# An attention and mixer kernel on one Trainium2 core: the second channel matrix of group 0 converted one run earlier, twenty unread products at the start, and two rewritten order tables

## The chip, the cores and the metric

The kernel runs on one core of a Trainium2 chip. The metric is device time in microseconds (us), the median of three executions. One further execution was recorded by the hardware profiler, and all rows below come from it. The engines are named as in the profile: PE is TensorE, DVE is VectorE, ACT is ScalarE, POOL is GpSimd, SP issues most of the DMAs.

## The reference

Rotary attention over 4 batches of 8 heads (576 rows, 64 dimensions, fp32), followed by a token mixer and a channel mixer:

```python
q_rot, k_rot = (rotate(q), rotate(k))              # 4 x 8 x 576 x 64
scores = scale * np.matmul(q_rot, k_rot.transpose(0, 1, 3, 2))
attn = np.exp(scores - max); attn = attn / (sum + 1e-09)
x = concat_heads(attn @ v)                         # 4 x 576 x 512
h = np.maximum(xt @ w_tok1, 0.0) @ w_tok2          # 576 -> 256 -> 576, float64 weights
u = x + h.transpose(0, 2, 1)
h2 = np.maximum(u @ w_ch1, 0.0) @ w_ch2            # 512 -> 1536 -> 512, float64 weights
return (u + h2).astype(np.float32)
```

## The kernel before, in words

**Attention.** Heads go in 16 pairs; pair n is prepared by `prep(n)`. The rows of k and q are loaded by SP, rotated in three operations (L437, L439, L443: on DVE for pair 0, in two parts; on POOL for the others), transposed on PE with the identity `ident` (L471, PSUM tiles `s`) and copied to `kt` and `qt` (L482). The scores (L593) take 288 of the 576 columns at a time; DVE finds the maximum (L493), ACT takes the exponential (L497), PE transposes the result (L616), L621 copies it to `pt`, L634 multiplies by v. The last 64 rows of two neighbouring pairs are done together as tails (L516 for their scores), so the tails of pairs 0 and 1 need both pairs' `kt` and `qt`. X and XT hold the attention's output, scaled at L668 and its neighbours.

**The mixers.** A float32 matrix that enters a product here is split into a high and a low part and multiplied three times. The weights arrive as float64 in 32-bit halves and are rebuilt by `f64_split`, one piece at a time: two ACT operations (L709, L711), a clamp L713 (DVE or POOL), L715, L717 and L719 on DVE, L721 and L723 (DVE or POOL), then L729 on ACT for the high and L730 (DVE or POOL) for the low part. The token mixer is L819 (first product), L824 and L827 (its result split into `rs`), L841 (second product) and L844 (addition to X); L791 and L793 split X into `xs` and `xt` ahead of it. The channel mixer works on four groups of 384 hidden columns. Each of five chunks of rows is transposed once (`up`: L910 on PE, ACT L915 gives `uh`, DVE L916 gives `ul`), and then for every group and chunk `cm1` (L936, then `gh` by ACT L938 and `gl` by DVE L940) and `cm2` (L963, added to X by DVE at L965). `cm1` needs the first matrix of its group (`c1h`, `c1l`), `cm2` the second (`c2h`, `c2l`).

**What sets the order.** The code records tasks with an engine, a model duration and their dependencies, and three calls of `plan.run` issue them. Run 1 (attention, the token weights, the token mixer of batch 0) follows the table `ORDER1`, one number for each task. Run 2 (the token mixers of batches 1 to 3, the first matrix of group 0, `up(0)` and `up(1)`) follows `ORDER2`. Run 3 (the second matrix of group 0, all other weights, `up(2)` to `up(4)`, `cm1`, `cm2`) is list-scheduled by the planner from its model durations. Each engine executes its own queue strictly in order. PSUM has eight banks, `s` in run 1 and `m` in runs 2 and 3; a product can start only when the reader before it has released its bank.

Of the kernel before, what the change touches and what calls it, by code (L numbers as in the profile page):

```python
# [64 lines left out]

class Task:
# [8 lines left out]
class Plan:  # L75
# [53 lines left out]
    def place(self, t, s, eng, dur, fn):  # L129
# [13 lines left out]
        fn()  # L143
# [3 lines left out]
        self.clock[eng] = end  # L147
# [64 lines left out]
AT = {'load': [1.46, -95.74, 1755.84, -446.16, -10.32, -39.47], 'rot': [-30.33, -28.71, -413.29, -24.98], 'pt': [2461.71, -120.88, 1877.09, 0.03], 'qk': [-19.92, -94.77, -29.81, -42.47, -64.18, 1974.42, -445.69, 27.95, -11.96, -66.6, -413.71, -4.28, -3.14, 1684.05, 2036.62, 1632.15, 1700.12, -3.39, -14.08, 1717.83], 'mx': [-18.32, -97.08, -28.47, -222.21, 6.35, 102.54, -32.49, -15.54, 1579.98, 1593.71, -66.46, 1669.44, -16.89, 1934.18, 1942.38, -85.25, -54.68, -66.81, 1912.69, -8.83, 1697.35, 2415.63, 1609.9, 23.08, -40.85, -271.23, 8.19, -10.94, -20.04, -405.36, -59.72, -406.05, 2099.98, 1.92, 1651.83, 1951.2, 1677.89, 1499.17, -7.34, 1632.2], 'ex': [-19.75, -25.79, -97.92, -19.73, 1983.61, 1573.24, -17.98, -1.23, -9.94, -101.57, 88.51, 1713.87, -29.01, 1630.6, -9.17, 1879.5, 1922.03, -18.78, -23.18, 19.55], 'tr': [-261.73, 1684.38, -347.64, 1853.57, -223.18, 1740.33, -18.09, 1625.16, -353.85, 2050.66, -65.51, 2482.09, -74.23, -25.76, 1924.68, -6.29, -550.16, 2116.11, -49.33, -19.36], 'cp': [-285.8, 1993.92, -15.28, -338.61, -33.12, -32.9, 1494.57, -414.57, -230.35, -354.01, -214.2, -9.85, -35.68, -247.66, -14.87, -307.76, -26.24, 90.92, 1865.89, 2189.31], 'pv': [1983.73, 10.91, -453.58, -23.11], 'p1': [-52.7, -56.83, 1864.91, -1.75], 'fin': [2216.99, -20.0], 'tok': [1652.21, 1875.86, 1482.41, 2166.22, -11.87, 1947.96], 'inv': [-8.92, -3.44], 'f6': [1767.81, 1652.44], 'tk': [1968.59, -7.94, -26.45, -12.06], 'pre': [-2.55], 'tm': [-283.71, 77.1, 1499.3, -17.97, 1601.75, -59.36, 1543.29, -96.53, -111.26, 1974.16, 1626.79, -49.74], 'wg': [1621.69], 'up': [3.65, 1617.77], 'ti': [5.61]}  # L212
ORDER1 = (
# [848 lines left out]
```

## Time and profile before

| | |
|---|---|
| device time, median of 3 | 602.62 us (602.53 to 603.88) |
| the profiled execution, device time | 602.69 us |
| its span in the trace | 600.9 us (1.8 us lie outside it) |
| PE busy | 585.6 us, 97% of the span |
| DVE, ACT, POOL busy | 385.3, 312.4, 309.3 us |
| run 1 to run 2 on PE | at 252.8 us |
| run 2 to run 3 on PE | at about 295 us |

The page of the profile gives busy time by engine, and the granted clock of PE. The view of waits sums PE's idle time by the instruction that ended it. The timeline lists starts and durations, and in brackets the idle time ahead of an instruction and its releaser. In this program a float32 product leaves two records for each instruction in the order, one for each pass; a transpose leaves one. Durations of single PE records overlap their neighbours, so what PE pays is the distance between starts.

### The profile page before, as it was taken

What the parts mean: (1) busy time and instruction counts of PE and PEld (TensorE: products, weight loads), DVE (VectorE), ACT (ScalarE), POOL (GpSimd) and SP (SyncE); (2) the same over time, 40 slices, a digit from 0 to 9 for tenths busy, and PEclk for the clock granted to TensorE, in tenths of its full rate; (3) what the DMA queues carried; (4) which work ended last, traced back from release to release, by engine and by line L of the source; (5) the groups of instructions that cost most, each with busy time, mean ns of one, the idle gap of its engine ahead of it and who ended that gap; (6) DMA issues with size and microseconds to landing.
All of it is one profiled execution on the core that took longest, in us unless ns stands there. A gap on an engine that the chain in (4) does not pass through costs nothing.

```text
span 600.9 us, 12684 instructions
## 1 busy us (share of the span) xinstructions
PE 585.6 (97%) x4825; PEld 461.0 (77%) x4825; DVE 385.3 (64%) x1121; ACT 312.4 (52%) x796; POOL 309.3 (51%) x258
## 2 busy tenths in 40 slices
PE   4999999999999999999999999999999999999997
PEld 3777676777677777687777888888888888888886
DVE  6998999998899988688845545445423443223232
ACT  3998999999999988243464332233202311110110
POOL 4997876888868531023578686477503760000000
PEclk9999999999999999999998999999999999999999
DMA  5443242313311201001122222122101200001123
GB/s 151 126 116 86 71 108 75 105 29 90 101 52 60 62 2 31 25 26 62 36 65 76 71 61 54 60 71 55 50 1 36 71 0 1 1 1 70 71 70 106
DMA packets 34093, 36.15 MB, mean 60 GB/s; under 512 B 13808, under 2 KB 27632, under 8 KB 34032
## 3 DMA queue, kind: packets, MB, share of 16 engines
q1 hardware_dynamic: 33200, 35.01, 20.3%
q8 instruction: 38, 0.62, 0.4%
q10 hardware_dynamic: 832, 0.33, 0.2%
q14 instruction: 23, 0.19, 0.1%
HBM read 30.61 MB, written 4.72 MB: 59 GB/s over the span
## 4 chain that ended last, share of the span: by engine, by line
PE 95%; DVE 2%; DMA 1%; ACT 1%; issue 0%; DVEq 0%
PE m L936 25%; PE m L963 24%; PE s L634 14%; PE s L593 11%; PE s L616 7%; PE m L841 3%; PE m L819 3%; PE s L471 2%; PE s L516 2%; PE s L819 1%; PE s L537 1%; PE s L663 1%; PE s L841 1%; DMA tabs<-in_tab_dram 1%; DVE p L493 0%; DMA kraw<-in_k_dram 0%
## 5 line engine op out<-in xcount | busy, mean ns | idle before, releaser
L938 ACT ACTIVATE gh<-m 128x512 fp32r<-128x512 f32 (+1 forms) x60 | 33.3, 555 | 174.0 <-PE m L936 170.8
L497 ACT ACTIVATE p<-p,nm 128x576 f32<-128x576 f32 x128 | 98.9, 778 | 1.7 <-DVE p L493 1.1
L940 DVE SCALAR_TENSOR_TENSOR gl<-m,gh 128x512 fp32r<-128x512 f32 (+1 forms) x60 | 38.1, 637 | 93.3 <-ACT gh L938 93.2
L965 DVE TENSOR_TENSOR X<-m,X 128x512 f32<-128x512 f32 (+1 forms) x65 | 44.4, 683 | 74.0 <-PE m L963 73.9
L936 PE MATMUL m<-uh,c1h 128*128 128x512 f32 (+1 forms) x240 | 89.1, 371 | 0.1
L936 PE MATMUL m<-ul,c1h 128*128 128x512 f32 (+1 forms) x240 | 88.9, 370 | 0.0
L936 PE MATMUL m<-uh,c1l 128*128 128x512 f32 (+1 forms) x240 | 88.9, 370 | 0.0
L634 PE MATMUL s<-pt,vraw 128*64 128x256 f32 (+1 forms) x640 | 84.7, 411 | 0.0
L963 PE MATMUL m<-c2l,gh 128*128 128x512 f32 (+1 forms) x219 | 84.6, 386 | 0.0
L963 PE MATMUL m<-c2h,gh 128*128 128x512 f32 (+1 forms) x219 | 84.6, 386 | 0.0
L963 PE MATMUL m<-c2h,gl 128*128 128x512 f32 (+1 forms) x219 | 84.6, 386 | 0.0
L593 PE MATMUL s<-kt,qt 64*128 64x288 f32 x512 | 80.9, 430 | 1.2 <-ACT kt L482 0.9
L721 POOL TENSOR_TENSOR fa<-fc,fa 128x512 f32<-128x512 f32 (+2 forms) x30 | 35.9, 1197 | 75.2 <-DVE fa L719 63.4
L634 PEld LDWEIGHTS s<-pt,vraw 128*64 128x64 f32 x640 | 43.1, 137 | 30.1 <-DVE p L493 1.3
L493 DVE TENSOR_SCALAR_CACHE_REDUCE p<-s,nm 128x288 f32<-128x288 f32 x128 | 62.3, 512 | 3.8 <-PE s L593 1.7
L621 ACT COPY pt<-s 128x320 f32<-128x320 f32 (+1 forms) x172 | 60.6, 408 | 4.9 <-PE s L616 3.4
L616 PEld LDWEIGHTS s<-ident,p 64*128 64x128 f32 x1152 | 47.0, 139 | 17.5 <-ACT p L497 8.1
L593 PEld LDWEIGHTS s<-kt,qt 64*128 64x128 f32 x512 | 51.1, 192 | 8.7 <-ACT pt L621 1.7
L493 DVE TENSOR_SCALAR_CACHE_REDUCE p<-s 128x288 f32<-128x288 f32 x128 | 53.9, 452 | 4.4 <-PE s L593 4.0
L713 POOL TENSOR_SCALAR fa<-fa 128x512 f32<-128x512 f32 (+3 forms) x30 | 50.9, 1699 | 9.5 <-ACT fa L709 9.4
L616 PE MATMUL s<-ident,p 64*128 64x64 f32 x1152 | 52.6, 226 | 0.3 <-ACT p L497 0.2
L936 PEld LDWEIGHTS m<-uh,c1h 128*128 128x128 f32 x240 | 45.5, 190 | 8.1 <-DVE ul L916 0.3
(130 smaller groups left out, 1061.8 us busy)
## 6 DMA issues: line engine op xcount, KB each, us to landing
stg<-in_moe_w_ch_dram SPq DMA_DIRECT2D x16, 384.0 KB, 3.2
stg<-in_moe_w_ch_dram SPq DMA_DIRECT2D x12, 512.0 KB, 3.7
vraw<-in_v_dram SPq DMA_DIRECT2D x16, 256.0 KB, 3.2
kraw<-in_k_dram SPq DMA_DIRECT2D x15, 256.0 KB, 3.2
qraw<-in_q_dram SPq DMA_DIRECT2D x15, 256.0 KB, 3.3
out_dram<-X SPq DMA_DIRECT2D x15, 256.0 KB, 2.3
stg<-in_moe_w_tok_dram SPq DMA_DIRECT2D x4, 512.0 KB, 4.3
kraw<-in_k_dram SPq DMA_DIRECT2D x32, 32.0 KB, 2.9
```

The source lines that it names most:

```text
L493: return lambda: nc.vector.tensor_scalar(out=p()[:, c * W2:(c + 1) * W2], in0=sb.t[:, 0:W2], scalar1=-D ** -0.5, scalar2=nm.t[:, 0:1] if c ...
L497: return lambda: nc.scalar.activation(out=p(), in_=p(), func=ACTF.Exp, bias=nm.t[:, 1:2], scale=-1.0, accum_out=l())
L593: nc.tensor.matmul(sbs[h].t[:, 0:W2], flat(qt.t)[halves[h], TL + j * P:TL + (j + 1) * P], flat(kt.t)[halves[h], TL * (1 - h) + u * W2:TL * ...
L616: nc.tensor.transpose(xy[z].t[:, i * TL:(i + 1) * TL], pb.t[halves[z], c0:c0 + P], ident[halves[z], halves[z]])
L621: return lambda: e(out=pt[c].t[:, R * h:R * h + m, o + z * TL:o + (z + 1) * TL], in_=xy[z].t[:, 0:m * TL].rearrange("p (r s) -> p r s", r=m))
L634: nc.tensor.matmul(ab.t[halves[h], 0:w], vb.t[:, h, r, :], m, start=(r == 0), stop=(r == R))
L713: clamp = lambda e: lambda: e.tensor_scalar(out=A(), in0=A(), scalar1=EXP_LO, scalar2=EXP_HI, op0=ALU.max, op1=ALU.min)
L721: mul_ = lambda e: lambda: e.tensor_tensor(out=A(), in0=C(), in1=A(), op=ALU.mult)
L936: nc.tensor.matmul(tb.t[:, 0:n], a, m, start=(i == 0), stop=(i == len(lst) - 1))
L940: y = add("DVE", dve(n), lambda f=f, tb=tb: nc.vector.scalar_tensor_tensor(out=gb.t[1][:, f, 0:n], in0=tb.t[:, 0:n], scalar=0.0, in1=gb.t[ ...
L963: nc.tensor.matmul(tb.t[:, 0:w], a, m, start=(i == 0), stop=(i == len(lst) - 1))
L965: y = add("DVE", dve(w) + 0.08, lambda u=u, tb=tb, cols=cols, w=w: nc.vector.tensor_tensor(out=u[:, cols], in0=tb.t[:, 0:w], in1=u[:, cols ...
```

## The change

Four things are changed in what runs, and a fifth is added that does not run.

- `make_identity` is called ahead of the POOL fills of `vraw`, `oT` and `pq` instead of behind them.
- A function `warm(n, w)` issues 2n products of the identity with itself into PSUM banks 7 and 6; nothing reads them. `warm(10, P)` is called ahead of the first `prep`. A second call stands inside the closure `tr` under a condition on `nm`. The closure is executed after the loop over `nm`, when `nm` is `"v"`, so the condition is never met.
- `weights(0, ..., (2,), held)`, the conversion of group 0's second matrix (three pieces), is recorded ahead of `plan.run(ORDER2)` instead of behind it. `ORDER2` grows from 162 to 195 entries, and run 3 has 33 tasks fewer and is scheduled anew.
- `ORDER1` is another permutation of the same 1666 tasks, and `ORDER2` is rewritten.
- Code that can merge two PSUM banks (`Half`, `duo`, `mx1`, `cq1`, `cp1`, `f51`) is added. It acts on the numbers in `MERGED`, and `MERGED` is empty.

```diff
+MERGED = ()
 ORDER1 = (
-    68, 84, 0, 16, 88, 8, 20, 24, 28, 36, 4, 92, 12, 96, 104, 40, 44, 48, 76, 100, 52, 64, 72, 60, 80, 108, 112, 116, 148, 156, 152, 32, 56, 1408, 1428,
+    68, 0, 84, 16, 20, 88, 24, 92, 96, 100, 28, 12, 4, 8, 40, 32, 44, 104, 48, 52, 64, 60, 56, 72, 80, 76, 36, 1464, 108, 112, 116, 120, 132, 128, 1472,
...
+        make_identity(nc, ident)
         for _, _, t in raw["v"].free:
             nc.gpsimd.memset(t[TL:P, 0, R, :], 0.0)
...
-        make_identity(nc, ident)
+
+        def warm(n, w):
+            for i in range(2 * n):
+                z = halves[i % 2]
+                nc.tensor.matmul(banks.tile[:, 7 - i % 2, 512 - w:512], ident[z], ident[z, 0:w], start=True, stop=True)
...
+                        if n == 0 and nm == ("q" if r0 == 0 else "k"):
+                            warm(2, TL)
...
+        warm(10, P)
         for n in range(NP):
             prep(n)
...
             ups[ci] = up(ci, AT["up"][ci])
+        weights(0, AT["wg"][0] + 1000, (2,), held)
         plan.run(ORDER2)
...
         held[0].users -= 1
-        weights(0, 1000, (2,), held)
         for ci in range(2, NC):
             ups[ci] = up(ci, 1000 + 100 * ci - 120)
```

How many instructions of each line an engine has is the same on PE but for the twenty products. Lines of the changed kernel are higher by 33 to 72: L471 is L504 there, L593 is L648, L616 is L674, L516 is L566, L910 is L982, L916 is L988, L936 is L1008, L963 is L1035, L965 is L1037, and L715, L717, L719 are L787, L789, L791.

The first rows on PE, before (the numbers behind names are buffers; `uk` and `uq` are the rotated rows of pair 0, `p` the exponentials):

```order
L471 MATMUL s<-ident,uk_105 128x64 x4
L471 MATMUL s<-ident,uq_106 128x64 x4
L471 MATMUL s<-ident,uk_105 128x64 x6
L593 MATMUL s<-kt_109,qt_112 128x288 x6
L471 MATMUL s<-ident,uq_106 128x64 x6
L593 MATMUL s<-kt_109,qt_112 128x288 x2
L616 MATMUL s<-ident,p_115 128x64 x8
L593 MATMUL s<-kt_109,qt_112 128x288 x8
```

and now:

```order
L415 MATMUL s<-ident 128x128 x20
L504 MATMUL s<-ident,uq_106 128x64 x4
L504 MATMUL s<-ident,uk_105 128x64 x10
L648 MATMUL s<-kt_109,qt_112 128x288 x2
L504 MATMUL s<-ident,uq_106 128x64 x6
L648 MATMUL s<-kt_109,qt_112 128x288 x12
L504 MATMUL s<-ident,uk_105 128x64 x10
L648 MATMUL s<-kt_109,qt_112 128x288 x2
```

Twenty products stand ahead of the first transposes, and the other rows up to the first tails (L516, now L566) are the same in number, in another sequence.

On PE in run 3, where the transposes of chunks 2 to 4 begin (eighty in a row in both kernels), before:

```order
L936 MATMUL m_3981<-ul_3992,c1h_3985 128x512
L936 MATMUL m_3981<-uh_3991,c1l_3986 128x512
L910 MATMUL m_3984<-ident,XT_63 128x64
L910 MATMUL m_3983<-ident,XT_63 128x64
L910 MATMUL m_3984<-ident,X_61 128x64
```

and now:

```order
L1035 MATMUL m_4004<-c2h_4007,gh_4413 128x512
L1035 MATMUL m_4004<-c2l_4008,gh_4413 128x512
L1035 MATMUL m_4004<-c2h_4007,gl_4414 128x512
L982 MATMUL m_3999<-ident,XT_63 128x64
L982 MATMUL m_4000<-ident,XT_63 128x64
L982 MATMUL m_3999<-ident,X_61 128x64
```

The eighty transposes stood behind `cm1` of chunks 0 and 1; now `cm2` of chunks 0 and 1 stands between, and they come 72 products later.

On DVE at the same place, before:

```order
L940 SCALAR_TENSOR_TENSOR gl_4361<-m_3981,gh_4360 128x512
L916 TENSOR_TENSOR ul_3994<-m_3984,uh_3993 128x8x64
L717 SCALAR_TENSOR_TENSOR fh_70<-stg_66,fa_68 128x512
L916 TENSOR_TENSOR ul_3994<-m_3983,uh_3993 128x8x64
L719 TENSOR_SCALAR fa_68<-fh_70 128x512
L916 TENSOR_TENSOR ul_3994<-m_3980,uh_3993 128x8x64
L916 TENSOR_TENSOR ul_3994<-m_3982,uh_3993 128x8x64
L916 TENSOR_TENSOR ul_3996<-m_3979,uh_3995 128x8x64
```

and now:

```order
L1037 TENSOR_TENSOR X_60<-m_4002,X_60 128x512
L1037 TENSOR_TENSOR X_60<-m_4004,X_60 128x512
L789 SCALAR_TENSOR_TENSOR fh_69<-stg_65,fa_68 128x512
L988 TENSOR_TENSOR ul_4014<-m_3999,uh_4013 128x8x64
L988 TENSOR_TENSOR ul_4014<-m_4000,uh_4013 128x8x64
L988 TENSOR_TENSOR ul_4014<-m_3998,uh_4013 128x8x64
L988 TENSOR_TENSOR ul_4014<-m_4003,uh_4013 128x8x64
L988 TENSOR_TENSOR ul_4016<-m_3997,uh_4015 128x8x64
```

Two conversion steps stood between the first three `ul`; now one stands ahead of the first, and eight `ul` follow without a break.

## Rows read from the trace of the kernel before

**Rows 1.** The page, busy us (share of the span) and instructions of each engine.
```profile
PE 585.6 (97%) x4825; PEld 461.0 (77%) x4825; DVE 385.3 (64%) x1121; ACT 312.4 (52%) x796; POOL 309.3 (51%) x258
```

**Rows 2.** PE's waits: releaser, us in total, times, longest us.
```profile
PE s L471 <- DVE uk L443: 7.2, 2, 6.0
PE m L910 <- DVE ul L916: 1.7, 3, 0.9
PE m L819 <- DVE X L668: 1.3, 1, 1.3
```

**Rows 3.** Timeline of the start: start us, us, engine, line, output, count, idle before.
```profile
5.99 0.48 PE L471 MATMUL s<-ident,uk 64*128 64x64 f32 x4 [5.99 <-DVE uk L443]
...
9.35 1.81 PE L593 MATMUL s<-kt,qt 64*128 64x288 f32 x6 [0.87 <-ACT kt L482]
...
10.31 1.54 POOL L437 TENSOR_TENSOR w<-kraw,tabs 128x640 f32<-128x640 f32 x1 [7.58 <-DMA kraw<-in_k_dram]
...
18.05 1.55 POOL L443 TENSOR_TENSOR uq<-uq,w 128x640 f32<-128x640 f32 x1
...
19.80 0.75 PE L471 MATMUL s<-ident,uq 64*128 64x64 f32 x10
...
20.66 0.49 DVE L482 COPY qt<-s 128x320 f32<-128x320 f32 x1 [0.18 <-PE s L471]
...
21.26 1.20 PE L516 MATMUL s<-kt,qt 64*64 64x288 f32 x16
```

**Rows 4.** PE records of L593 from 9 to 14 us, and from 14.3 to 16.
```profile
L593 PE MATMUL s<-kt,qt x16: 684/684/847, 9.3 to 13.3; 64*128 64x288 f32 x16
...
L593 PE MATMUL s<-kt,qt x13: 402/402/507, 14.4 to 15.9; 64*128 64x288 f32 x13
```

**Rows 5.** Timeline where run 1 ends on DVE and run 2 begins on PE.
```profile
251.05 1.27 DVE L844 TENSOR_TENSOR X<-s,X 128x512 f32<-128x512 f32 x2
...
252.80 0.70 PE L819 MATMUL m<-xs,w1h 128*128 128x512 f32 x2 [1.27 <-DVE X L668]
```

**Rows 6.** Windows of run 2 (252.8 to 292.8 us): busy time by engine, summed over four.
```profile
sum 40.00, PE 40.00 PEld 32.18 DVE 34.17 ACT 16.51 POOL 11.40; mean PE 10.00 PEld 8.05 DVE 8.54 ACT 4.13 POOL 2.85
```

**Rows 7.** DVE groups of 252.8 to 330 us: busy us, mean ns of one, idle before.
```profile
L793 DVE TENSOR_TENSOR xs<-X,xs 128x512 fp32r<-128x512 f32 x9 | 6.9, 779 | 0.7 <-ACT xs L791 0.6
...
L791 DVE CAST xs<-X 128x512 fp32r<-128x512 f32 x6 | 2.6, 425 | 1.8 <-PE m L819 1.7
...
L715 DVE TENSOR_SCALAR fa<-fa 128x512 uint32<-128x512 uint32 x3 | 2.0, 680 | 1.1 <-POOL fa L713 1.1
...
L717 DVE SCALAR_TENSOR_TENSOR fh<-stg,fa 128x512 uint32<-128x512 uint32 x3 | 2.0, 682 | 0.0
...
L719 DVE TENSOR_SCALAR fa<-fh 128x512 uint32<-128x512 uint32 x3 | 1.2, 419 | 0.0
```

**Rows 8.** Timeline of the eighty transposes in run 3 and what DVE does meanwhile.
```profile
311.58 0.28 PE L910 MATMUL m<-ident,XT 64*128 64x64 f32 x2
...
312.31 0.69 DVE L940 SCALAR_TENSOR_TENSOR gl<-m,gh 128x512 fp32r<-128x512 f32 x1 [1.32 <-ACT gh L938]
...
313.56 0.68 DVE L717 SCALAR_TENSOR_TENSOR fh<-stg,fa 128x512 uint32<-128x512 uint32 x1
...
314.75 0.42 DVE L719 TENSOR_SCALAR fa<-fh 128x512 uint32<-128x512 uint32 x1
...
315.09 4.99 DVE L916 TENSOR_TENSOR ul<-m,uh 128x512 fp32r<-128x512 f32 x10
...
317.02 0.19 PEld L936 LDWEIGHTS m<-uh,c1h 128*128 128x128 f32 x1 [0.27 <-DVE ul L916]
```

**Rows 9.** Windows about that place: us, PE busy (records), granted clock, DMA share, GB/s.
```profile
314.00:317.70 3.70, 1.87 (x18) 1.00 0.44 111
317.80:321.10 3.30, 3.30 (x9) 0.50 0.00 0
321.20:325.00 3.80, 3.80 (x18) 1.00 0.39 104
```

More of the change, by code (lines that the diff above doesn't have):

```diff
@@ L63, in t, with __init__ @@
         return self.held[2]
+class Half:
+    def __init__(self, buf, z):
+        self.buf = buf
+        self.z = z
+    @property
+    def t(self):
+        return self.buf.t[:, self.z]
 class Task:
@@ L142, in place @@
                 b.slots.taken += 1
-        fn()
+        if fn:
+            fn()
+        else:
+            end = -1e9
         t.end, t.eng = end, eng
@@ L146, in place @@
             self.mode = t.mode
-        self.clock[eng] = end
+        self.clock[eng] = max(self.clock[eng], end)
         if eng == "DVE" and t.port:
@@ L392, in attention, with duo, none @@
             nc.gpsimd.memset(t[:, S:S + TL], 0.0)
-        make_identity(nc, ident)
+        def warm(n, w):
+            for i in range(2 * n):
+                z = halves[i % 2]
+                nc.tensor.matmul(banks.tile[:, 7 - i % 2, 512 - w:512], ident[z], ident[z, 0:w], start=True, stop=True)
         ready, ready_v, couple = {}, {}, {}
+        duos = [0]
+        def duo():
+            duos[0] += 1
+            if duos[0] - 1 in MERGED:
+                b = Buf(banks, True)
+                return b, [Half(b, 0), Half(b, 1)]
+            return None, [Buf(banks), Buf(banks)]
+        def none(deps, bufs):
+            return add("DVE", 0.0, None, deps, bufs)
         order_tr = [None]
@@ L461, in prep @@
                                  for z0, z1 in ((0, R + 1),)]
-                    xy = [Buf(banks), Buf(banks)]
+                    one, xy = duo() if n else (None, [Buf(banks), Buf(banks)])
                     split = r0 > 0
@@ L472, in tr, with cq1 @@
                                                     ub.t[halves[z], r].rearrange("p h d -> p (h d)"), ident[halves[z], halves[z]])
+                        if n == 0 and nm == ("q" if r0 == 0 else "k"):
+                            warm(2, TL)
                     pp = pos + AT["pt"][2 * odd + int(2 * pr)] if n else FIRST + r0
                     t = add("PE", 0.06 * (r1 - r0) + 0.012, tr, x, [*xy, ub, tb], pp, mode="row")
-                    for z in range(2):
+                    if one:
+                        def cq1(e, one=one, tb=tb, m=R + 1):
+                            return lambda: e(out=tb.t.rearrange("p (r z) s -> p z r s", z=2)[:, ::-1],
+                                             in_=one.t[:, :, 0:m * TL].rearrange("p z (r s) -> p z r s", s=TL))
+                        done += [none([t], [one, tb]), both(cq1, 2 * (R + 1) * TL, [t], [one, tb], pp)]
+                    for z in range(0 if one else 2):
                         m = r1 - r0 - (z and split)
@@ L509, in tails @@
             t = []
+            sb2, ones = score_banks()
             for u in range(2):
[L511 removed]
+                sbs = sb2[u]
                 def qk(sbs=sbs, u=u):
@@ L523, in tails @@
                 x = None
-                for u in range(2):
+                if ones[h]:
+                    none([t[0][0]], [ones[h], nms_[h], pbs[h]])
+                    x = add("DVE", 0.68, mx1(ones[h], nms_[h], p), [t[1][0]], [ones[h], nms_[h], pbs[h]])
+                for u in range(0 if ones[h] else 2):
                     x = add("DVE", 0.44 if u else 0.38, mx(t[u][1][h], nms_[h], p, u), [t[u][0], x], [t[u][1][h], nms_[h], pbs[h]],
@@ L600, in pair @@
                     x = None
-                    for u in range(2):
+                    if ones[h]:
+                        none([t[0][0]], [ones[h], nmb[h], pb])
+                        x = add("DVE", 0.68, mx1(ones[h], nmb[h], p), [t[1][0]], [ones[h], nmb[h], pb])
+                    for u in range(0 if ones[h] else 2):
                         x = add("DVE", 0.44 if u else 0.38, mx(t[u][1][h], nmb[h], p, u), [t[u][0], x], [t[u][1][h], nmb[h], pb], g + AT["mx"][20 * odd + 4 * i + 2 * u + h])
@@ L608, in pair @@
                 for h in range(2):
-                    xy = [Buf(banks), Buf(banks)]
+                    one, xy = duo()
                     m = R + h
@@ L618, in pair, with cp1 @@
                     x = order_tr[0] = add("PE", 0.06 * m + 0.006, tr, [*xs[0:h + 1], order_tr[0]], [*xy, pb, pt[c]], at("tr", h), mode="row")
-                    for z in range(2):
+                    if one:
+                        def cp1(e, one=one, c=c, o=o, h=h, m=m):
+                            return lambda: e(out=pt[c].t[:, R * h:R * h + m, o:o + P].rearrange("p r (z s) -> p z r s", z=2),
+                                             in_=one.t[:, :, 0:m * TL].rearrange("p z (r s) -> p z r s", r=m))
+                        ev[c] += [none([x], [one, pt[c]]), both(cp1, 2 * m * TL, [x], [one, pt[c]], 0.0)]
+                    for z in range(0 if one else 2):
                         def cp(e, z=z, xy=xy, c=c, o=o, h=h, m=m):
@@ L653, in pair @@
             tinv, rt = tail_inv[n]
-            xy = [Buf(banks), Buf(banks)]
+            one, xy = duo()
             cs = hp * 2 * D
@@ L675, in f6, with f51 @@
                                             in1=rt.t[0:TL, c:c + 1].to_broadcast([TL, D]), op=ALU.mult)
-                x_done.setdefault(b, []).append(add("DVE", dve(R * D), f5, [x, inv], [xy[z], rb], pf))
+                def f51():
+                    nc.vector.tensor_tensor(out=X[b][:, :, cs:cs + 2 * D].rearrange("p r (z d) -> p z r d", z=2),
+                                            in0=one.t[:, :, 0:R * D].rearrange("p z (r d) -> p z r d", r=R),
+                                            in1=rb.t[:, 0:R].rearrange("p r z -> p z r").unsqueeze(3).to_broadcast([P, 2, R, D]), op=ALU.mult)
+                if one and not z:
+                    x_done.setdefault(b, []).append(none([x, inv], [one, rb]))
+                else:
+                    x_done.setdefault(b, []).append(add("DVE", dve(2 * R * D) if one else dve(R * D), f51 if one else f5, [x, inv], [xy[z], rb], pf))
                 def f6a(z=z, c=c):
```

20 lines of the change are left out of this document (14 added, 6 removed), and 145 rows, old and new, of tables (ORDER1, ORDER2).

## The prediction

> **What bounds the kernel now.** The page's first part comes first: TensorE is busy for 585.6 of the 600.9 us of the span [rows 1]. About 15 us are left, and any gain from a new order lies in them or in time in which TensorE works at half its clock. The view of waits says where they are [rows 2]: 7.2 us until the first rotated rows of k arrive, 1.7 us among the transposes of the chunks in run 3, 1.3 us where run 1 hands over to run 2. The rest are waits below 1 us and the end of the program, which the change leaves alone. The other engines are busy for little more than half the span. They matter only where TensorE waits for one of them, so I go through these three places, and then through run 2, where the change adds work.
>
> **The start.** The twenty products cost TensorE time only if they end after the first transposes could start, at 5.99 us [rows 3]. A score product has 288 columns and leaves two records. Six records of pairs take 1.81 us and the first of a pair lasts 0.85 [rows 3, 4], so pairs start (1.81 - 0.85) / 2 = 0.48 us apart. For 128 columns that is 0.48 x 128 / 288 = 0.21 us, and twenty products, which leave forty records in twenty pairs, take about 4.3 us. The identity is built first on POOL, from about 0.7 us, and has two short operations, so the products run from about 1.4 to 5.7. The first transposes now take `uq` first, which is ready about 0.3 us after `uk`. The products cost nothing; if I have the pairs wrong and they take twice as long, they end at 10.0 instead of 5.7, and the first transposes are 3.8 us late.
>
> What can they bring? [...] POOL rotates pair 1's k and q from 10.31 in six operations of 1.55 us, until 18.05 + 1.55 = 19.60; their transposes begin at 19.80, the last copy of `qt` is at 20.66 + 0.49 = 21.15, and the tail scores L516 start at 21.26 [rows 3]. POOL waits for the DMA of pair 1's k, which stands at the same place of SP's queue in both kernels. All that TensorE has ahead of L516 is the same in both orders, so it gets there earlier only to wait: at most 21.26 - 21.15 = 0.11 us, and another 0.18 if that copy no longer waits for its transposes. POOL's two identity operations, moved ahead of the fills, do not delay the first rotation, since it waits for the DMA at 10.31. I take -0.1, with -0.3 and 0 as ends.
>
> [...]
>
> **The handover from run 1 to run 2.** DVE's last additions to X end at 251.05 + 1.27 = 252.32 and TensorE begins at 252.80, after 1.27 us of idle [rows 5]. The changed order ends with the same three reads of `s` on DVE, so I take 0, with 0.3 either way. Inside run 1 the stalls of TensorE between 22 and 252 us add up to about 1 us. A new permutation of the same tasks can save at most that, or add as much: 0, with 0.8 either way.
>
> **Run 2, the cover.** TensorE is busy for 40.00 of 40 us, DVE for 34.17, ACT for 16.51, POOL for 11.40 [rows 6]. The three pieces of the second matrix bring work here that was in run 3. From the counts in the two orders, DVE gets three more L713, one L715, three L717, three L719, one L723 and one L730, and gives four L791 and one L793 to the others. By rows [rows 7], with 0.42 for a one-operand step (L719's row; L713 on DVE has none of this size), 0.68 for L715, L717 and, having no row of its own size, L723, and 0.78 for L730 (L793's row, also a subtraction): 1.26 + 0.68 + 2.05 + 1.26 + 0.68 + 0.78 = 6.7, less 4 x 0.425 + 0.78 = 2.5, so 4.2 us more. DVE idles 40.00 - 34.17 = 5.8 us here. It fits, narrowly, and the pieces stand late in DVE's queue with the adds to X and the splits ahead of them. Nobody needs the matrix until `cm2`, which waits for two `cm1`, some 16 us. Cost 0. If the cover is gone (next to last part) it is up to 4.2.
>
> **Run 3, the eighty transposes.** In both kernels the transposes of chunks 2 to 4 come in one row, and they need all eight PSUM banks and four again. Before, they begin at 311.58 and the next L936 starts at 317.02, 5.44 us later, waiting for the fifth `ul` [rows 8]. DVE sets that: `gl` starts 0.73 us after the begin, a `ul` at 312.95, L717, a `ul`, L719, and ten `ul` in 4.99 us from 315.09 (the last four are half as large). One `ul` comes every 0.60 us, and the third of these is the fifth of all: 315.09 + 3 x 0.60 = 316.9, just ahead of 317.02. After the change DVE has the addition of the last `cm2` (it needs no ACT, and can start about 0.11 after the begin, 0.6 earlier than `gl`), one L789, and eight `ul` in a row. With starts 0.62 to 0.70 apart for the first two and 0.60 then, the first `ul` starts at 1.4 and the fifth ends at about 1.4 + 5 x 0.60 + 0.1 = 4.5 us after the begin. Gain 5.44 - 4.5 = 0.9; I take -0.85. If L789's input from POOL or L787 is late there is no gain (0); if L789 runs ahead of the addition, it is up to -1.2.
>
> **The clock after it.** From 314.0 to 317.7 TensorE is busy for 1.87 of 3.70 us, and from 317.8 to 321.1 the granted clock is 0.50, the lower level [rows 9]. Eight or nine records of L936 run in these 3.3 us where they would take half, so the fall costs about 1.65 us. After the change the pause is a sixth shorter, and its work is the same. I leave the fall in, on the likelier side, since the row before it has much the same shape.
>
> [...]
>
> **Sum,** against the profiled execution's own 602.69 (0.07 above the median): -0.1 - 0.85 + 0 + 0 + 0 = -0.95, so 601.74; the median of the changed kernel should be about 601.7. Its own range, by the ends given, is 600.6 to 602.8.
>
> **Rivals.**
>
> - The clock does not fall after the shorter stretch. Speaks for it: the idle shrinks by 0.9 of the roughly 1.8 us in the window. Against it: the eighty transposes and the waits between them stay in one stretch. It gives -0.95 - 1.65 = -2.6, so 600.1.
> [...]
> - Slower: in run 2 DVE becomes the engine that sets the pace. Its work rises from 34.2 to 38.4 of 40 us. Where a split of X (`xs`, `rs`) stands behind a conversion step, it is late by that step, and TensorE has no other work of its queue to do. It decides from the point at which DVE's steps inserted ahead of a split exceed DVE's idle time up to there; in the worst case the whole 4.2 us appear as waits: 602.69 - 0.95 + 4.2 = 605.9, more likely half of it, 603.8. Also counted here is a worse run 1 order, with 1 to 2 us more of stalls.
> - The change does not do what it says: the second call of `warm` is never executed and the merging is empty, which the rows of the order show. Should the first call do nothing either and the burst keep its length, the time is 602.6.
>
> **How the numbers follow.** A measurement of this kernel tells from no change what is over about 0.3%, 1.8 us. Chances: the forecast 0.52, the clock kept 0.22, the start in full 0.06, slower as told 0.13, no effect at all 0.07. Faster by over 0.3% means below 600.8: the clock kept (nearly all of 0.22), the start (0.06), and the low tail of the forecast (0.05), 0.33. Slower by over 0.3% means above 604.4: the worse half of the slower rival and a little more, 0.10. The rest, 0.57, is within 0.3%. For 8 in 10 the range reaches from 599.8, past the kept clock, to 603.6, past no effect and the milder half of the slower rival.
>
> **What would show it.** Right: in the start, twenty products end before 6 us and L566 starts at 20.9 to 21.3, with a new wait ahead of it if the scores are faster. At the transposes of run 3, now about 327 us, 4.5 us between the first L982 and the next L1008, without a conversion step between the `ul`. Behind them a stretch of 3.3 us at 0.50. In run 2, TensorE without waits for DVE over 0.3 us. Wrong: a wait of L891 or L913 for L863, L865 or L899 in run 2, which is the slower rival; a granted clock of 1.00 after the transposes, which is the first; or L566 starting ahead of 20 us, which says that POOL's chain was not what held it.

## The result: 611.84 us, slower, and where the nine microseconds are

The changed kernel takes 611.84 us (median of four executions, 609.89 to 613.16) against 602.58 for the kernel before (four executions, 601.98 to 603.88): a ratio of 1.0148, 95% interval 1.0112 to 1.0184. The forecast was 601.7, range 599.8 to 603.6. The profiled execution took 613.16 us, the slowest of the four; its span is 611.4. One execution of a kernel below took 731.37 us at a granted clock of 0.755 and one of the kernel before 1171.43 us; both are left out of the medians.

The page of the changed kernel, busy us by engine, beside [rows 1]:

```profile
span 611.4 us, 12791 instructions
...
PE 593.5 (97%) x4865; PEld 464.9 (76%) x4865; DVE 390.8 (64%) x1118; ACT 313.9 (51%) x797; POOL 309.2 (51%) x260
```

TensorE is busy for 7.9 us more. 4.64 of these are the forty records of the unread products, which fill time that was idle before; about half of the rest, 1.6, is what the stretch at the lower clock below costs (an estimate: half of its 3.20 us). A share of 97% in both kernels says nothing of the loss. Its waits do (releaser, us in total, times, longest), beside [rows 2]:

```profile
PE s L566 <- DVE p L533: 1.8, 1, 1.8
PE m L891 <- DVE xt L865: 1.6, 1, 1.6
PE s L415 <- POOL ident masks.py:199: 1.3, 1, 1.3
PE s L504 <- DVE uk L476: 1.1, 1, 1.1
PE s L504 <- POOL uq L476: 1.0, 1, 1.0
PE m L913 <- DVE X L916: 1.0, 1, 1.0
PE s L648 <- ACT kt L522: 0.9, 1, 0.9
PE m L891 <- DVE XT L916: 0.9, 1, 0.9
PE s L674 <- ACT pt L684: 0.8, 1, 0.8
...
PE m L982 <- DVE ul L988: 0.7, 2, 0.3
```

The big wait at the start is gone, since the products fill it, the wait among the transposes (L982) is 0.7 instead of 1.7, and, besides the 1.3 for the identity at the start, eight waits are new or longer, between 0.5 and 1.8 us, on DVE, POOL and ACT. Cut at the start of the first token product of run 2 (L819, now L891) and of the first `cm1` (L936, now L1008), the two profiled executions compare so, in us:

| | run 1, up to | run 2 | from the first `cm1` to TensorE's last record |
|---|---|---|---|
| before | 252.80 | 42.37 | 302.35 |
| changed | 260.82 | 45.68 | 301.43 |
| difference | +8.0 | +3.3 | -0.9 |

The three add up to 10.4 us, more than the 9.3 between the medians, since the profiled execution of the changed kernel lies above its median.

**Run 1.** The dearest place, a timeline of the changed kernel (start us, us, engine, line; in brackets the idle time ahead and its releaser):

```profile
157.19 1.03 DVE L785 TENSOR_SCALAR fa<-fa 128x512 f32<-128x512 f32 x1
...
158.52 1.39 DVE L789 SCALAR_TENSOR_TENSOR fh<-stg,fa 128x256 uint32<-128x256 uint32 x1
...
159.59 1.71 POOL L470 TENSOR_TENSOR w<-kraw,tabs 128x640 f32<-128x640 f32 x1
159.94 1.91 DVE L865 TENSOR_TENSOR xt<-XT,xt 64x512 fp32r<-64x512 f32 x1
...
161.86 0.46 DVE L533 TENSOR_SCALAR_CACHE_REDUCE p<-s 128x288 f32<-128x288 f32 x1
...
162.82 2.10 PE L566 MATMUL s<-kt,qt 64*64 64x288 f32 x14 [1.76 <-DVE p L533]
```

Three steps on DVE that nobody is waiting for stand ahead of the maxima L533, and each is two to three times as long as at its shortest: 1.39 for L789 on 256 columns, where the same step in the kernel before takes 0.44, and 1.91 for L865, where 0.69 is its shortest. L785 takes 1.03, where 0.42 is its shortest at this size, and before it ran on POOL at this place: `ORDER1` is not only another sequence. A number's remainder by four says which of a task's engines runs it, and 166 of the 1666 tasks go to another engine than before (13 in `ORDER2`). No run separates the sequence from this choice. L865 begins while POOL's L470 runs, and ends 0.55 us after L470 has (159.59 + 1.71 = 161.30; 159.94 + 1.91 = 161.85). Behind the wait, TensorE's clock falls, as the windows show (us, PE busy, granted clock, DMA share, GB/s):

```profile
162.00:163.00 1.00, 0.18 (x4) 0.99 0.00 0
163.10:166.30 3.20, 3.20 (x34) 0.50 0.00 0
166.50:169.00 2.50, 2.50 (x30) 1.00 0.00 0
```

**Run 2.** The windows of 260.8 to 300.8 us, busy us summed over four, beside [rows 6], and the timeline where the largest waits are:

```profile
sum 40.00, PE 37.32 PEld 29.27 DVE 36.88 ACT 19.90 POOL 14.90; mean PE 9.33 PEld 7.32 DVE 9.22 ACT 4.97 POOL 3.73
```

```profile
287.91 1.34 POOL L795 TENSOR_TENSOR fh<-fh,fa 128x384 f32<-128x384 f32 x1
...
288.31 1.50 DVE L789 SCALAR_TENSOR_TENSOR fh<-stg,fa 128x512 uint32<-128x512 uint32 x1
...
289.22 1.74 POOL L865 TENSOR_TENSOR xs<-X,xs 128x512 fp32r<-128x512 f32 x1
...
289.84 1.40 DVE L791 TENSOR_SCALAR fa<-fh 128x512 uint32<-128x512 uint32 x1
...
291.16 1.87 DVE L916 TENSOR_TENSOR X<-m,X 128x512 f32<-128x512 f32 x3
291.89 0.73 PE L913 MATMUL m<-rs,w2h 128*128 128x512 f32 x2 [1.02 <-DVE X L916]
...
294.97 0.99 POOL L802 TENSOR_TENSOR c1l<-fh,c1h 128x384 fp32r<-128x384 f32 x1
295.10 1.42 DVE L865 TENSOR_TENSOR xt<-XT,xt 64x512 fp32r<-64x512 f32 x1
296.57 0.50 PE L891 MATMUL m<-xt,w1th 128*128 128x512 f32 x1 [1.64 <-DVE xt L865]
```

DVE is busy for 36.9 of 40 us and, near the end, without a break. L789 and L791 of the second matrix take 1.50 and 1.40 us where [rows 7] have 0.68 and 0.42, the additions L916 are queued behind them, and TensorE waits for the banks that these release. The pattern is the one of run 1: L789 ends 0.56 us after L795 on POOL, L791 0.28 after L865 there, L865 on DVE 0.56 after L802.

**Run 3.** The eighty transposes, beside [rows 8, 9]:

```profile
339.23 0.28 PE L982 MATMUL m<-ident,XT 64*128 64x64 f32 x2
339.34 0.69 DVE L1037 TENSOR_TENSOR X<-m,X 128x512 f32<-128x512 f32 x1 [1.35 <-PE m L1035]
...
340.60 4.87 DVE L988 TENSOR_TENSOR ul<-m,uh 128x512 fp32r<-128x512 f32 x8
...
343.74 0.69 PE L1008 MATMUL m<-uh,c1h 128*128 128x512 f32 x1
...
343.90:347.20 3.30, 3.30 (x8) 0.50 0.02 5
```

From 339.23 to 343.74 is 4.51 us, where it was 5.44, and the lower clock follows, as before.

### The profile page after: what moved, and what is told of

Its sections match the earlier page's. It is cut to its first block, busy times and chain, and to the rows that moved or that the text cites. A ratio compares the mean times of both kernels' runs of the same rounds, so it can differ in the third digit from the quotient of the medians.

```text
span 611.4 us, 12791 instructions
## 1 busy us (share of the span) xinstructions
PE 593.5 (97%) x4865; PEld 464.9 (76%) x4865; DVE 390.8 (64%) x1118; ACT 313.9 (51%) x797; POOL 309.2 (51%) x260
## 4 chain that ended last, share of the span: by engine, by line
PE 50%; DVE 3%; ACT 0%; POOL 0%; issue 0%; ACTq 0%
PE m L1008 24%; PE m L1035 24%; PE m L913 1%; DVE ul L988 1%; DVE fh L789 1%; DVE xs L865 0%; PE m L891 0%; DVE fa L791 0%; DVE xt L865 0%; DVE XT L916 0%; DVE X L916 0%; PE m L982 0%; ACT xs L863 0%; POOL fa L793 0%; POOL fh L795 0%
## 5 line engine op out<-in xcount | busy, mean ns | idle before, releaser
L1008 PE MATMUL m<-uh,c1h 128*128 128x512 f32 (+1 forms) x240 | 89.0, 371 | 0.1
L1008 PE MATMUL m<-ul,c1h 128*128 128x512 f32 (+1 forms) x240 | 89.0, 371 | 0.0
L1008 PE MATMUL m<-uh,c1l 128*128 128x512 f32 (+1 forms) x240 | 88.8, 370 | 0.0
L1037 DVE TENSOR_TENSOR X<-m,X 128x512 f32<-128x512 f32 (+1 forms) x65 | 44.4, 684 | 68.8 <-PE m L1035 68.7
L1035 PE MATMUL m<-c2l,gh 128*128 128x512 f32 (+1 forms) x219 | 84.6, 386 | 0.0
L1035 PE MATMUL m<-c2h,gh 128*128 128x512 f32 (+1 forms) x219 | 84.6, 386 | 0.0
L1035 PE MATMUL m<-c2h,gl 128*128 128x512 f32 (+1 forms) x219 | 84.5, 386 | 0.0
L648 PE MATMUL s<-kt,qt 64*128 64x288 f32 x512 | 81.0, 427 | 1.6 <-ACT kt L522 0.9
L793 POOL TENSOR_TENSOR fa<-fc,fa 128x512 f32<-128x512 f32 (+3 forms) x32 | 37.6, 1175 | 69.6 <-DVE fa L791 67.1
L533 DVE TENSOR_SCALAR_CACHE_REDUCE p<-s,nm 128x288 f32<-128x288 f32 x128 | 61.9, 512 | 3.6 <-PE s L648 2.1
L674 PEld LDWEIGHTS s<-ident,p 64*128 64x128 f32 x1152 | 45.8, 140 | 19.6 <-ACT p L545 6.7
L684 ACT COPY pt<-s 128x320 f32<-128x320 f32 (+1 forms) x160 | 55.5, 407 | 6.5 <-PE s L674 5.5
L648 PEld LDWEIGHTS s<-kt,qt 64*128 64x128 f32 x512 | 50.9, 192 | 9.8 <-ACT pt L684 1.4
L533 DVE TENSOR_SCALAR_CACHE_REDUCE p<-s 128x288 f32<-128x288 f32 x128 | 53.9, 452 | 5.5 <-PE s L648 4.1
L674 PE MATMUL s<-ident,p 64*128 64x64 f32 x1152 | 51.7, 228 | 2.7 <-ACT pt L684 0.8
L785 POOL TENSOR_SCALAR fa<-fa 128x384 f32<-128x384 f32 (+3 forms) x27 | 45.0, 1669 | 15.3 <-ACT fa L781 15.3
L1008 PEld LDWEIGHTS m<-uh,c1h 128*128 128x128 f32 x240 | 45.6, 190 | 8.1 <-DVE ul L988 0.3
```

The lines of the kernel that those rows point to most:

```text
L533: return lambda: nc.vector.tensor_scalar(out=p()[:, c * W2:(c + 1) * W2], in0=sb.t[:, 0:W2], scalar1=-D ** -0.5, scalar2=nm.t[:, 0:1] if c ...
L648: nc.tensor.matmul(sbs[h].t[:, c0:c0 + W2], flat(qt.t)[halves[h], TL + j * P:TL + (j + 1) * P], flat(kt.t)[halves[h], TL * (1 - h) + u * W ...
L674: nc.tensor.transpose(xy[z].t[:, i * TL:(i + 1) * TL], pb.t[halves[z], c0:c0 + P], ident[halves[z], halves[z]])
L684: return lambda: e(out=pt[c].t[:, R * h:R * h + m, o + z * TL:o + (z + 1) * TL], in_=xy[z].t[:, 0:m * TL].rearrange("p (r s) -> p r s", r=m))
L785: clamp = lambda e: lambda: e.tensor_scalar(out=A(), in0=A(), scalar1=EXP_LO, scalar2=EXP_HI, op0=ALU.max, op1=ALU.min)
L793: mul_ = lambda e: lambda: e.tensor_tensor(out=A(), in0=C(), in1=A(), op=ALU.mult)
```

## The experiments

Each kernel is compared with executions of the kernel before that stood beside it (medians 602.34 to 602.58). Three cuts of each trace serve throughout, as in the table above: the length of run 1, of run 2, and of run 3 to TensorE's last record. Line numbers shift by a few from kernel to kernel; a line is named with its number in the kernel spoken of.

### One part at a time

**The new ORDER1 alone,** in the kernel before:

```diff
 ORDER1 = (
-    68, 84, 0, 16, 88, 8, 20, 24, 28, 36, 4, 92, 12, 96, 104, 40, 44, 48, 76, 100, 52, 64, 72, 60, 80, 108, 112, 116, 148, 156, 152, 32, 56, 1408, 1428,
+    68, 0, 84, 16, 20, 88, 24, 92, 96, 100, 28, 12, 4, 8, 40, 32, 44, 104, 48, 52, 64, 60, 56, 72, 80, 76, 36, 1464, 108, 112, 116, 120, 132, 128, 1472,
...
```

> The kernel before with the changed ORDER1 and nothing else: no products at the start, the second matrix converted in run 3 as before. Theory (the new sequence of run 1 makes TensorE wait): run 2 begins on TensorE some 7 to 8 us later than the 252.8 us of before, with the wait of the tail scores for DVE at about 161 us, and the end is 7 to 8 us later, about 610. Rival (the products at the start, or what the earlier conversion does, delay run 1): run 2 begins within 1 us of before and the time is within 1 us of 602.6.

Measured: 608.27 us (606.24 to 609.77), ratio 1.0095 (1.0063 to 1.0127). Run 1 lasts 259.31 us, run 2 42.37, exactly as before. The largest waits inside run 1 are those of the changed kernel:

```profile
PE s L516 <- DVE p L493: 1.8, 1, 1.8
...
PE s L616 <- ACT pt L621: 0.8, 1, 0.8
...
PE s L616 <- DVE p L493: 0.5, 1, 0.5
```

The theory holds in its place, and is a little high in the size: 6.5 us in run 1 instead of 7 to 8, of which 1.7 is a stretch at the lower clock near 22 us. The wait of 1.77 us at 162.7 is there without any product at the start and without the conversion. The fall of the clock behind it is not: from 162.7 to 166.0 the granted clock is 1.00 here. Nor does it fall after the eighty transposes, and run 3, the same as before, lasts 300.76 us instead of 302.35.

**The conversion in run 2 alone** (the new ORDER2 and the moved call, the old ORDER1):

```diff
+        weights(0, AT["wg"][0] + 1000, (2,), held)
         plan.run(ORDER2)
...
-        weights(0, 1000, (2,), held)
```

> The kernel before with the second matrix of group 0 converted in run 2, by the changed ORDER2; ORDER1 as before, no products. Theory (DVE and POOL, with the conversion, delay steps that TensorE waits for in run 2): run 1 as before, run 2 longer by 3 to 4 us with waits of L819 and L841 for DVE, 0.9 us back at the eighty transposes, so 604.5 to 606. Rival (run 2 suffers only from what run 1 leaves unfinished): run 2 as long as before, 42.3 us, and 601.7.

Measured: 603.77 us (603.29 to 605.07), ratio 1.0022 (1.0009 to 1.0034). Run 1 252.58, run 2 45.85 (3.5 longer), run 3 301.43 (0.9 shorter). The two waits are the ones of the changed kernel, 1.7 for `xt` and 1.1 for X:

```profile
PE m L820 <- DVE xt L794: 1.7, 1, 1.7
PE m L820 <- DVE X L669: 1.3, 1, 1.3
PE m L842 <- DVE X L845: 1.1, 1, 1.1
```

So run 2's loss does not come from what run 1 leaves behind. The time is lower than expected: nine of its ten executions had a granted clock of 0.999 or 1.000, and most of those of the kernel before did not (see the last section). Against those of the kernel before at 0.999 (601.12 to 601.65 us) the loss is about 2.4, near to the 3.5 less 0.9 of the profile.

**The products alone** (identity first, then the twenty products):

> The kernel before with the identity built first and the twenty unread products at the start, nothing else. Theory (POOL's rotation of pair 1 bounds the start): the first score records are faster, but the tail scores L516 start between 20.9 and 21.3 us, and the time is 602.2 to 602.6. Rival (the products bring the faster clock and it counts): 600.3. Second rival (they are late or lower the clock afterwards): over 603.5.

Measured: 602.44 us (601.53 to 603.79), ratio 1.0006 (0.9993 to 1.002): no difference. The windows of its start (us, PE busy, granted clock, DMA share, GB/s), the last two records of the products, and the tail scores:

```profile
5.60:8.90 3.30, 1.29 (x18) 1.00 0.52 143
9.00:12.30 3.30, 3.21 (x16) 0.50 0.71 193
12.40:20.00 7.60, 6.84 (x89) 1.00 0.69 186
...
5.55 0.27 PE L398 MATMUL s<-ident 64*128 64x128 f32 x2
...
20.94 0.96 PE L521 MATMUL s<-kt,qt 64*64 64x288 f32 x12
```

The forty records take 4.48 us, a pair every 0.21, which is the lower level (0.48 x 128 / 288 by the slow score pairs of [rows 3, 4]); most last 0.42 us, the last two 0.27. The four transposes at 5.95 us take 0.34 and the six at 7.82 take 0.40, where the kernel before has 0.48 at 5.99 [rows 3] and 0.58 at 7.89. From these durations I estimate that the clock rises at about 5.5 us, when the products are nearly over, and is still up at 7.8, with TensorE busy for 1.29 of the 3.30 us to 8.90. In the window from 9.0 us, just where the scores begin, the granted clock is 0.50; from 12.4 us it is 1.00, and before, the score records shorten from 684 to 402 ns at about 14.0 [rows 4]. L521, the tail scores, begin 0.3 us earlier than in [rows 3].

**The changed kernel with the old ORDER1:**

> The changed kernel with the ORDER1 of before, all else as changed. Theory (the three parts add up, and ORDER1 is the largest): the changed time less 7 to 8 us, about 604 to 605, equal to the kernel with the conversion alone less 0.3. Rival (the parts amplify each other): 608 or more.

Measured: 605.08 us (603.88 to 606.21), ratio 1.0046 (1.0031 to 1.0061). Run 1 253.01, run 2 45.85. Against the changed kernel's 611.84 the old ORDER1 brings 6.8 us back. The parts add up roughly: 5.7 (ORDER1) + 1.2 (conversion) - 0.1 (products) = 6.8 of the 9.3 by medians. The rest is not taken apart; in it are the wait of 1.0 us at 40.8 (below), which the kernel with ORDER1 alone does not have, and the granted clock, which differs between executions by more than some of these parts.

### Run 1: which step of the new order does it

**Three DVE steps moved behind the tails' maxima,** in the changed kernel; L785, L789 and L865 of the timeline above are three entries of ORDER1:

```diff
 ORDER1 = (
-... 6340, 4560, 4564, 6388, 4504, 1132, 1136, 1140, 6352, 6548, 4132, ...
+... 6340, 4560, 4564, 4504, 1132, 1136, 1140, 4132, ...
...
-... 4680, 4676, 4684, 4465, ...
+... 4680, 4676, 4684, 6388, 6352, 6548, 4465, ...
```

> The changed kernel with three entries of ORDER1 moved later: the DVE steps L785 and L789 of the token weights and the split L865 of xt at 157 to 162 us stand behind the maxima of the tails. Theory (these three, held up behind POOL's rotation, made TensorE wait 1.76 us for DVE at 162.8): the wait falls below 0.4 us, the granted clock stays at 1.00 around 163 us, run 2 begins at 257.5 to 259.2 instead of 260.8, the median is 609 to 610. Rival (DVE as a whole is late there): the wait stays, or moves to another place within 10 us, and the time stays at 611 to 612.

Measured: 609.05 us (608.18 to 609.87). Run 1 lasts 257.39 us, 3.4 less; no wait over 0.15 us and no fall of the clock is left between 154 and 257 us. Three entries out of 1666 were worth 3.4 us of the profiled span, 2.8 by medians: 1.76 of waiting and about 1.6 for the lower clock behind it. The wait is shown to come from them; that the clock falls behind it is not, since the same wait stood without a fall in the kernel with ORDER1 alone.

**Pair 2's k loaded ahead of the token weights,** on top of the last one:

```diff
-... 184, 188, 272, 268, 6284, 220, 232, 236, 240, 6240, ...
+... 184, 188, 232, 236, 240, 272, 268, 6284, 220, 6240, ...
```

(of the entries between, only those that SP issues).

> The changed kernel with the three steps moved as in the run where DVE's steps stand behind the tails' maxima, and with the three loads of pair 2's k moved up in SP's queue ahead of the token weights. Theory (POOL idles 2.50 us at 21.8 for pair 2's k, which lands late behind two transfers of 512 KB, and all its later rotations are late by that, so that TensorE waits 1.05 us for uq at 40.8): the idle of POOL falls below 0.8 us, the wait at 40.8 falls below 0.3 us, run 2 begins 0.8 to 1.3 us earlier than 257.4, the median is about 608. Rival (POOL's order of rotations, not the load, delays uq): POOL's idle goes, the wait at 40.8 stays, 609.

In the changed kernel POOL stands idle for 2.50 us, waiting for that load; before, its six operations ended at 19.60 [rows 3] and the next began at 19.77:

```profile
21.83 1.55 POOL L470 TENSOR_TENSOR w<-kraw,tabs 128x640 f32<-128x640 f32 x1 [2.50 <-DMA kraw<-in_k_dram]
```

Measured: 609.55 us, run 1 257.81, and the wait for `uq` at 41.5 us is still 1.03. The first theory fell as I had set it up, but not in the rival's way either. POOL's idle only moved from k to q:

```profile
POOL w L471 <- DMA kraw<-in_k_dram: 7.3, 1, 7.3
POOL w L471 <- DMA qraw<-in_q_dram: 3.1, 1, 3.1
```

The last 64 rows of pair 2's q are issued at 20.0 us, behind two loads of 512 KB and three of v. **So that load was moved as well** (entry 276 behind 268):

> As the run with pair 2's k loaded ahead of the token weights, and now the last load of pair 2's q (64 rows, 32 KB) also ahead of them: POOL's 2.50 us of idle had only moved there, to 3.06 us for q at 25.5. Theory (POOL's first rotations are late behind the loads, and TensorE's wait of 1.03 us for uq at about 41 follows from it): POOL has no wait for a DMA over 1 us after 10 us, the wait at 41 falls below 0.3 us, and run 2 begins near 256.6 instead of 257.4 to 257.8. Rival (POOL has enough other work, and uq's place in its order decides): the wait at 41 stays at about 1 us.

Measured: 607.58 us (606.85 to 610.21), run 1 256.19, 1.2 us less than with the three DVE steps alone. POOL's only wait for a DMA after its first start is 0.67 us, and the wait for `uq` is gone; a wait of 0.6 us for a maximum stands at 40.5 in its place. The order of the loads in the first 20 us costs less than these 1.2 us: 0.53 of them lie ahead of the tail scores (L567 begins at 21.42 there and at 20.89 here), where the profiled execution with the three steps alone has a granted clock of 0.50 for 6.8 us and this one for 3.4 (0.994 and 0.997 in the mean). Some 0.7 is left for the loads. The changed kernel also begins its tail scores at 20.89, so of the 8.0 us of run 1 the four moves together explain 4.6. Of the other 3.4, idle time of TensorE is 2.0 (from 22 us to the end of run 1 it is 3.60 us here and 1.61 in the kernel before), with 0.84 and 0.29 at 151 and 0.5 at 84 us in it. The last 1.4 is no wait in the profile: TensorE's records fill 230.59 us there instead of 229.19, at a granted clock of 1.00 in both, for the same work. Its cause is open.

### Run 2: the place of the conversion

**One split moved from POOL to DVE,** to see whether POOL's operation is what makes the DVE step long (entry 6949 to 6948: the same task's first alternative), in the kernel with the conversion alone:

> The kernel with the conversion alone moved to run 2, with one split L794 that runs on POOL at 281.17 us given to DVE. Theory (a DVE step that reads SBUF and begins while a POOL operation runs ends only some 0.3 to 0.6 us after that operation does): L720 at about 281.8 takes 0.4 to 0.5 us instead of 1.39, DVE pays 0.69 for the split, the wait of L842 falls by about 0.3 us, the time is within 0.7 of 603.8. Rival (those steps are long by themselves): L720 still takes 1.4 us and the wait of L842 grows by 0.7.

Measured: 604.24 us (602.92 to 606.3), ratio 1.0028. The same step, first with and then without POOL's L794 beside it (the second row is this kernel):

```profile
281.79 1.39 DVE L720 TENSOR_SCALAR fa<-fh 128x512 uint32<-128x512 uint32 x1
...
281.96 0.43 DVE L720 TENSOR_SCALAR fa<-fh 128x512 uint32<-128x512 uint32 x1
```

1.39 us became 0.43 when the operation beside it left POOL for DVE; L720 itself was not touched. The wait of L842 fell from 1.09 to 0.13, more than expected; the wait for `xt` grew from 1.67 to 1.92, because DVE now does the split. Run 2 is 45.27 us, 0.6 shorter; the medians, 604.24 and 603.77, tell no difference.

**Steps of the conversion moved behind the split of `xt`.** First L718, L720, L722, with the ACT step and the load that need their buffers (entries 7332, 7336, 7340, 7364 and 7356 behind 6956):

> The kernel with the conversion alone moved to run 2, with three DVE steps of the first piece of the second matrix (L718, L720, L722), a load and an ACT step moved behind the split of xt of the last batch. Theory (these steps, held up by POOL, stand ahead of the adds L845 and the split L794 for which TensorE waits 1.09 and 1.67 us): both waits fall below 0.4 us, run 2 is about 2.5 us shorter, and the median is 601 to 601.6 instead of 603.8. Rival (DVE is simply full in run 2): the waits move to the next adds or splits and the time stays within 0.7 of 603.8.

Measured: 607.92 us, run 2 49.71. Both waits went, and a single one of 4.08 us took their place: the next piece's load was issued later, DVE waited 4.21 us for ACT's step on it, and the additions were queued behind. This kernel did not test what it was built for. So then only L720 and L722, without the load:

> The kernel with the conversion alone moved to run 2, with only the DVE steps L720 and L722 of the first piece of the second matrix, and the ACT step that needs their buffer, moved behind the split of xt; L718 stays, so that the next load is issued as early as before (in the kernel with all three moved that load came 3.8 us later and DVE waited 4.21 us for the next piece). Theory (DVE steps ahead of the adds and the split): the waits of 1.09 and 1.67 us fall below 0.4 us each, no wait above 1 us takes their place, run 2 ends about 2.4 us earlier, median 601 to 602. Rival (DVE full in run 2): the waits move, 603 to 605.

Measured: 607.82 us (606.26 to 608.56), run 2 48.58. Again both waits fell, to 0.00 and 0.14, and again another took their place:

```profile
PE m L842 <- ACT uh L916: 2.0, 1, 2.0
...
287.02 0.67 ACT L712 ACTIVATE fc<-stg 128x512 f32<-128x512 uint32 x1 [6.45 <-DVE fa L722]
```

ACT's L712 waits 6.45 us for the buffer that the moved L722 releases, and `rs` and `uh`, for which TensorE waits, are queued behind it on ACT. Both kernels then run at the lower clock for 6.8 us, 291.8 to 298.6 and 290.7 to 297.5, with TensorE busy for 5.3 and 6.4 of it. Half of that busy time, an estimate of what the lower clock costs there, is about 2.7 and 3.2 us, most or all of the 3.9 and 2.7 by which their run 2 is longer than the 45.85 of the conversion alone. Here the rival was right that the waits move, but not in its reason (a full DVE) nor in its time (603 to 605): taken one by one, the steps move the wait to another queue.

**All 33 tasks of the conversion behind the old ORDER2:**

```diff
 ORDER2 = (
     6688, 6692, 7056, 7060, ..., 7048, 7052, 7229,
+    7312, 7316, 7324, 7328, ..., 7436, 7441,
```

> The kernel before, with the second matrix of group 0 recorded for run 2, but its 33 tasks appended behind the 162 of the old ORDER2 instead of placed among them. Theory (the place of the conversion's DVE steps ahead of the adds and splits costs the time in run 2, not the conversion itself): run 2 as before, 42.3 us, no new wait of L820 or L842 for DVE. With the matrix ready, the planner no longer puts eighty transposes in a row, so most of the 3 us that TensorE idles there go too, and the lower clock after them, 1.7 us: 598 to 600. Rival (DVE can't carry the work in this stretch wherever it stands): TensorE waits for the matrix or for banks at the first cm2, 602.5 or more.

Measured: 600.42 us (600.04 to 601.28), ratio 0.9971 (0.9959 to 0.9984): faster than the kernel before. Run 2 lasts 42.39 us, as before, and run 3 299.70. Its waits:

```profile
PE s L472 <- DVE uk L444: 7.0, 2, 6.0
PE m L820 <- DVE X L669: 1.3, 1, 1.3
PE s L594 <- ACT kt L483: 0.9, 1, 0.9
PE m L911 <- DVE ul L917: 0.6, 1, 0.6
PE s L594 <- ACT pt L622: 0.3, 1, 0.3
```

The conversion now lies beside the first two `cm1`, where DVE has time, the planner puts 32 transposes ahead of the first `cm2` and 48 later, and the clock stays up in the profiled execution (1.000 in the mean). Against the executions of the kernel before beside it with a granted clock of 0.999 (601.25 to 601.47) the gain is about 0.9 us; the rest of the 2.2 goes with fewer falls of the clock. The rival (DVE can't carry it) fell.

**The same with the products and the identity first,** that is, both ideas of the change with neither of its tables:

> The changed kernel with the old ORDER1, and with the conversion's 33 tasks behind the 162 of the old ORDER2: both ideas of the change, neither of its rewritten tables. Theory (the ideas cost nothing, the tables do): 600.0 to 600.6, the same as without the twenty products within 0.5. Rival (the products cost something in themselves, the lower clock that follows them included): over 601.

Measured: 599.78 us (599.49 to 601.3), ratio 0.9963 (0.9953 to 0.9974), the lowest median of this study. The ideas of the change are sound or harmless; with its two tables they take 12.1 us more (611.84).

## Why the prediction was wrong

**Inside run 1: "0, with 0.8 either way".** This is the step that failed, by 8.0 us. The argument was that the stalls of TensorE before, about 1 us, bound what a new permutation can do. They bound only what it can save. What it can add has no such bound, and I had looked at the start and the end of run 1 in the new order and not at what stands ahead of the maxima in between. In the list of rivals it was "1 to 2 us more of stalls", without a place. The timeline above shows the dearest place: L865 stands directly ahead of the maxima that release L566. From 22 us to the end of run 1 TensorE's idle time rose from 1.61 to 5.91 us, 1.6 to 1.7 went to the lower clock, and about 2 us to records that are busy for longer, whose cause stays open. "The same tasks" was not quite so either: 166 of them changed engine, L785 among them.

**Run 2: "it fits, narrowly … cost 0".** Wrong by 3.3 us. The term of 4.2 us was made of durations without POOL beside DVE. It also counted one additional L715 where run 2 has three (seven instead of four on DVE); with 0.68 for each it is 5.6 of the 5.8 us that DVE had idle. In the changed kernel the two big steps take 1.50 and 1.40 us instead of 0.68 and 0.42, and DVE's busy time in four windows rises by 2.7 us (36.9 against 34.2; over the whole of run 2 by 6.5, 42.58 of 45.68 against 36.08 of 42.37), while the waits come to 1.64 + 1.02 us at the end of the stretch. That DVE fits on average did not help: its work near the end is in one row without a gap. The slower rival named this mechanism, its engine and its lines, and priced it between 2.1 and 4.2; measured 3.3. That the size fits is partly luck, since neither the two uncounted L715 nor the time that POOL held DVE were in it. It was given 0.13, and stood for the whole case of a slower kernel.

**Run 3: right.** The addition ahead of one L789 and then eight `ul`: 4.51 us, forecast 4.5; the gain 0.93, forecast 0.85 to 0.9.

**The start: right in place, nearly in size.** The products end at 5.98 us and L566 begins at 20.89, forecast 20.9 to 21.3, with waits of 0.73 and 0.72 us ahead of it. That is 0.37 earlier than before, just past the end of 0.3, and POOL's last rotation of pair 1 ends at 19.33 instead of 19.60. That the products bring the faster clock to the first scores, no run shows: with the products alone the granted clock is 0.50 from 9.0 to 12.3 us, where the scores run, and in the changed kernel 0.56. Nor did the start pay in full, which had 0.06 in the chances: the median with the products alone is 602.44 us beside 602.56.

**The handover: right within 0.4.** The wait is 0.87 instead of 1.27 us.

**The clock after the transposes: the wrong question.** I gave the kept clock 0.22, as if the fall belonged to the kernel. The same eighty transposes with the 4.5 us behind them stand in nine of the profiled kernels, the changed one among them: three show the fall and six do not. With 5.4 to 5.5 us behind them two of three show it.

**The second call of `warm` and the merging** do nothing, as forecast: the forty records are all that TensorE has more (4865 against 4825).

## What to carry to other kernels

The idle time of a queue bounds what a new order can save there, never what it can cost; before a rewritten table is forecast at zero, go through the in-order queue of the engine that releases the critical one, and look for long steps ahead of short ones that somebody waits for. Price a step on DVE with what runs on POOL beside it, not with its shortest row: here the same step took 0.43 and 1.39 us. Work that has no early reader goes behind the others in every queue that it uses; moved step by step it blocked a buffer and so the next queue.

## What the runs showed of the hardware

**A DVE step that reads SBUF can be held by an operation of POOL.** In the pairs of rows above a DVE step that began beside a POOL operation ended 0.28 to 0.56 us after it, and the experiment with one split moved shows that the POOL operation is the cause: L720 took 1.39 us with L794 on POOL beside it (281.17 to 282.90) and 0.43 without. The maxima (L493, L533), whose input is PSUM, lasted 0.45 to 0.52 us beside POOL's rotations. The steps with two inputs (L789, L865) ended 0.12 to 0.16 us earlier than their shortest rows (0.44, 0.68, 0.69), put behind the end of the POOL operation, would; the one-operand L720 and L791 ended 0.28 after it, with shortest rows of 0.43 and 0.42, so 0.14 to 0.15 earlier. By these rows, and as my estimate, nearly the whole step comes after the POOL operation; what in the chip makes it wait, no run shows. I had not weighed such meetings in the prediction; worked out from the rows, three of them in run 2 cost (1.50 - 0.68) + (1.40 - 0.42) + (1.42 - 0.69) = 2.5 us, and the two waits there come to 2.7.

**The lower clock comes in some executions and not in others.** The executions of the kernel before that stood beside the first four experiments fall into groups by their mean granted clock: at 0.999 six took 601.12 to 601.65 us, at 0.996 or 0.997 thirteen took 602.18 to 603.04, at 0.994 four took 603.61 to 603.81. In the mean clock each step is about what one more stretch like that of 343.90 to 347.20 above takes from it (half of 3.3 us in 601, 0.003); the times step by 1.1 to 1.2 us. Which stretch it was is known of the profiled executions alone. The kernel with the conversion alone had 0.999 or 1.000 in nine of ten, and the one with all 33 tasks appended 1.000 in five of six. Kernels with and without the products are not compared by this number: before the first change of the clock that a profile records, its column reads 1.00, over slow records too (9.3 to 13.3 us in [rows 4]). A difference below 2 us between two single executions of such a kernel is read with the granted clock beside it.
